# First two pairs' carry and values in smaller steps, third pair's loads moved ahead of the second weights, every order anew

## The chip, the cores and the metric

The kernel runs on one core of a Trainium2 chip. The core has five engines that run side by side: TensorE (PE, matmuls; PEld is its weight load), VectorE (DVE), ScalarE (ACT), GpSimd (POOL) and SyncE (SP). SP and GpSimd issue DMAs. Times are device microseconds (us); lower is better. The kernel before takes 174.0 us, the median of three runs (173.99 to 175.69).

## What is computed

Inputs are q, k, v and alpha, each of 4 batches, 8 heads, 768 positions and 48 dimensions, and two weights, w_in (384 x 2048) and w_out (2048 x 384). The first half is a recurrence with a decay:

```python
for t in range(S):
    state = alpha[:, :, t, :, None] * state + einsum('bhd,bhe->bhde', k[:, :, t], v[:, :, t])
    y[:, :, t] = einsum('bhd,bhde->bhe', q[:, :, t], state)
```

Its output, 3072 tokens of 384, goes through a two-layer network: `h = x @ w_in; g = relu(h) ** 2; out = g @ w_out`.

## The kernel before

**Tiles.** Positions are cut into chunks of 128, and two chunks make a pair (256 positions of one batch, all heads). There are 12 pairs, three to a batch. Within a chunk, two neighbouring positions share a partition (i = 0, 1), so a chunk has 64 rows of two.

**A pair's stages, with the lines of the profile.** `loads` (L609, or L605 on GpSimd's queue) fetches alpha, k, q and v into RAW. `decay` takes the logarithm of alpha (ACT), sums it along the positions by matmuls with triangular ones, and takes the exponential of plus and minus the sums (asb); DVE multiplies q and k with it into QKS. For pairs 0 and 1 this is `decay_half`, in two halves of four heads (X = 0, 1): L675, L681, L693, L696; the others use L632 to L663. `values` casts v to bf16 into VBF (L624). `turned` transposes QKS into QKT: pairs 0 and 1 by halves on TensorE (L747), with an eviction by ACT (L758) or DVE (L761); pairs 2 and 3 in one piece (L715, L720); pairs 4 to 11 by a DMA (L727). `scores` multiplies q and k of a chunk (L777) into four banks (i, X); DVE multiplies each with the causal mask into PMB (L797), or ACT first evicts it to SBUF (L790) and DVE masks from there (L792). `carry` builds the state after each chunk: a matmul of k and v (L816), then DVE or GpSimd adds the old state and applies the chunk's decay (L831, L834, L837) into SBF. `mixed` makes the pair's output: the values, that is the masked scores times v (L856, the function `mm`, 48 matmuls for all heads), then the products of the old state (`before`, in two steps), then the eviction into XT (L903 by ACT, L900 by DVE). Pairs 4 to 11 use `mixed_back` (L932, L942) and a transposing DMA.

**The network.** `up` has eight steps per pair (u = 0 to 7): six matmuls of 256 columns (L985), relu on ACT (L995), the square on DVE into GT (L997). `down` has eight steps per pair, two halves of 128 tokens by four parts of four matmuls of 384 columns (L1018); after the fourth part ACT evicts (L1025) and a DMA stores. The last half of the last pair is `last_down` (L1037). `up` alternates between two PSUM banks (psH); the first WIDE steps, counted over all pairs, also take one of the two banks of `down` (psO). GT has three buffers.

**What sets the order.** Each stage has a number in TABLE, to which twice the pair's index is added; this is its priority. A planner in the program (`Program.order`) goes through the work engine by engine with costs written into each `add`, and of the operations that are ready takes the one of the lowest number; its result is the fixed order of instructions of each engine. Every engine then waits by semaphores for what it needs. Operations with dependencies across engines name what they read and write. The planner also puts matmuls on nothing (L1004, tile WARM) into idle time of TensorE before the first down.

**DMA order.** SP loads the first two pairs: alpha, k, q, v of pair 0, then of pair 1. GpSimd's queue holds the weights, cut into pieces: five of w_in (two of 2, three of 4 blocks of 128 columns) and four of w_out. PARTS says how they are dealt out: the first run waits for pair 1's alpha, and QUEUED puts pair 2's four loads on the same queue behind the first run. In the kernel before, the first run is six pieces (all of w_in and the first of w_out), then pair 2, then three pieces of w_out. OPENS lets pair 3's first load wait for one named piece.

Of the kernel before, what the change touches and what calls it, by code (L numbers as in the profile page):

```python
# [16 lines left out]
    dict(decay0=-97.00571, decay1=-78.81219, turned0=-80.03886, turned1=-50.01967, scores0=-30.48193, scores1=-47.68772, carry=-27.42287, mixed=-10.34508, up=13.54943, down=5.38323, scale00=46.21211, scale01=15.6952, scale10=-43.7223, scale11=24.38742, ends=-0.19963, values=-0.27295, loads=-207.65325, pair=-201.56601, last=-192.65267),  # L17
    dict(decay0=-75.64812, decay1=-42.50964, turned0=-47.6396, turned1=-36.35059, scores0=-27.54796, scores1=-14.27818, carry=-27.02336, mixed=-9.92749, up=13.91788, down=5.77749, scale00=24.25062, scale01=-73.05864, scale10=28.44156, scale11=53.47468, ends=69.1898, values=-2.51561, loads=-194.30495, pair=-191.20832, last=-172.89529),
    dict(decay=-7.48475, turned=3.12884, scores0=9.47855, scores1=6.55405, carry=1.85699, mixed=10.59462, up=17.47201, down=3.43096, loads=-74.75818),
    dict(decay=9.05655, turned=9.43988, scores0=10.08163, scores1=11.32914, carry=10.39665, mixed=11.89133, up=17.92099, down=4.23853, loads=-73.80479),  # L20
    dict(decay=9.3345, turned=9.43988, scores0=11.74226, scores1=10.89073, carry=10.54465, mixed=12.03376, up=21.0863, down=1.87816, loads=-73.8231),
    dict(decay=8.7564, turned=9.67304, scores0=11.70712, scores1=12.0564, carry=10.89438, mixed=12.21007, up=21.29448, down=1.43236, loads=6.43356),
    dict(decay=8.69387, turned=9.58387, scores0=11.86871, scores1=11.0227, carry=10.77621, mixed=11.96308, up=21.05913, down=2.40841, loads=7.7569),
    dict(decay=9.23435, turned=10.31244, scores0=11.36545, scores1=11.31146, carry=10.85231, mixed=12.13782, up=22.61627, down=2.40841, loads=8.07049),
    dict(decay=9.1013, turned=10.6921, scores0=11.60211, scores1=13.72977, carry=10.17742, mixed=18.09191, up=22.49685, down=2.4227, loads=7.9898),
    dict(decay=9.1013, turned=10.66148, scores0=19.46122, scores1=19.67082, carry=16.52927, mixed=20.05528, up=26.04938, down=2.38036, loads=7.9898),
    dict(decay=17.68176, turned=18.97432, scores0=20.03114, scores1=21.47118, carry=18.7218, mixed=19.83455, up=26.32882, down=2.72559, loads=13.16964, masks=-27.17958),
    dict(decay=17.68176, turned=18.97432, scores0=20.03114, scores1=21.47118, carry=18.7218, mixed=19.83455, up=26.32882, down=2.72559, loads=13.16964),
]
POOLS = [dict(decay=1, turned=2, scores=2, carry=1, mixed=2), dict(decay=0, turned=1, scores=1, carry=1, mixed=0)]  # L30
# [12 lines left out]
XTS = ('DVE', 'DVE')  # L43
COPIED = ((1,), (2,))
TURNS = ('DVE', 'ACT')
# [385 lines left out]
def bass_gla_recurrent__then__act_relu_squared_kernel(  # L431
# [23 lines left out]
    KT = DM // 128  # L455
# [213 lines left out]
    def decay_half(g, X, at):  # L669

        r, l, a, x, c_ = g % NRAW, g % NLAB, g % NASB, g % NQK, g % NAC
        ps, key = bank(POOLS[g]["decay"])
# [59 lines left out]
    def turned_half(g, X, at):  # L732

        x, t = g % NQK, g % NQT
        if g == 0:
            spots = [bank(POOLS[g]["turned"]) for z in range(2)]
        else:
            spots = [bank(POOLS[g]["turned"])] * 2
# [27 lines left out]
    def scores(g, at, js=range(NP), late=0.0):  # L766
        t, m = g % NQT, g % NPM
        halves = sorted({j // 2 for j in js})
        banks = {(i, X): bank(POOLS[g]["scores"] if g < FIRST else 0) for X in halves for i in range(2)}
# [35 lines left out]
    def carry(g, at, spots=None):  # L805
        x, vb, c_ = g % NQK, g % NV, g % NAC
        first, final = g % NW == 0, g % NW == NW - 1
        chunks = [0] if final else [0, 1]
        banks = [pr.bank(spots or pools[POOLS[g]["carry"] if g < FIRST else 0]) for c in chunks]

        def mm(pe):
# [9 lines left out]
        add("PE", mm, 250, at, reads=[("qks", x, 0, X) for X in range(2)] + [("vbf", vb)],  # L821
            writes=[b[1] for b in banks], form=64, size=32 * len(chunks))
# [21 lines left out]
    def mixed(g, at, spots=None, between=None):  # L844
# [29 lines left out]
        def mm(pe):  # L874
            order = [[s for s in shares if s[1] % 2 == col] for col in range(2)]
            for y in range(2 * KT):
                for i in range(2):
                    for col in range(2):
                        h, n, off = order[col][y]
# [176 lines left out]
    for g in range(G):  # L1056
# [15 lines left out]
        if g - 1 not in RUNS:  # L1072
            stage(2 * g + o["carry"], lambda at, g=g: carry(g, at), "carry", g)
# [138 lines left out]
```

## Time and profile before

| | us |
|---|---|
| median of three runs | 174.0 |
| lowest and highest | 173.99, 175.69 |
| the profiled execution | 174.21 |
| its span, first to last instruction | 172.5 |
| TensorE busy | 167.6 |
| VectorE busy | 119.4 |
| ScalarE busy | 116.9 |
| GpSimd busy | 36.4 |

The granted TensorE clock is full in nearly the whole span. In the page's groups a line reads: source line, engine, operation, output and inputs by name, shapes, count; then the busy time of the group and the mean of one instruction; then the idle time of that engine ahead of these instructions and what ended it. In an answer in order of time, the first number is the start, the second the length. The chain of work that ended last is followed back from the last instruction to what released each step.

### The profile page before, as it was taken

The page shows a single profiled execution, that of the slowest core. Times are in us where ns is not written, and L with a number is a line of the kernel's source. Part 1 is how long each engine was busy: PE and PEld are TensorE (multiplying, and loading weights), DVE is VectorE, ACT ScalarE, POOL GpSimd, SP SyncE. Part 2 cuts the span into 40 slices and gives each one's busy share as a digit, 9 for nine tenths or more (in the row PEclk, how much of TensorE's full clock was granted, in tenths as well). Part 3 has the DMA queues.
Part 4 walks back from the last instruction along what each step waited for, and adds up shares of the span by engine and source line. Part 5 has one row for each costly group of instructions (what it writes and reads, how often), then busy time and mean ns, then how long its engine had stood idle before and what let it go on. Part 6 is the DMA issues. An engine that isn't in the chain of part 4 may idle for free.

```text
span 172.5 us, 6016 instructions
## 1 busy us (share of the span) xinstructions
PE 167.6 (97%) x2611; PEld 123.9 (72%) x2611; DVE 119.4 (69%) x257; ACT 116.9 (68%) x236; POOL 36.4 (21%) x63
## 2 busy tenths in 40 slices
PE   7889999999999999999999999999999999999994
PEld 7457687757777786777777777777776867877763
DVE  7887958964999999578897698289784804423300
ACT  2887679546989685568993794669973556657621
POOL 4079600100012001010142122320512310202220
PEclk9999999999999999999999999999999999999999
DMA  5999999999994999999999999999929343112122
GB/s 138 323 304 171 206 324 238 157 270 287 308 327 113 230 217 261 144 305 196 323 203 234 218 207 252 236 231 332 186 50 160 72 62 62 22 25 49 40 51 91
DMA packets 76314, 32.89 MB, mean 191 GB/s; under 512 B 69632, under 2 KB 75456, under 8 KB 76288
## 3 DMA queue, kind: packets, MB, share of 16 engines
q1 hardware_dynamic: 70384, 25.04, 65.0%
q0 software_dynamic: 5904, 7.47, 21.8%
q8 instruction: 20, 0.33, 0.8%
q14 instruction: 6, 0.05, 0.1%
HBM read 25.17 MB, written 4.72 MB: 173 GB/s over the span
## 4 chain that ended last, share of the span: by engine, by line
PE 95%; DVE 2%; issue 1%; ACT 0%
PE psH L985 36%; PE psO L1018 36%; PE psG L777 4%; PE psO L1004 3%; PE psG L856 2%; PE psG L942 2%; PE psG L816 2%; PE psO L1037 2%; PE psG L932 2%; PE psO L985 2%; DVE qks L696 2%; PE psG L642 1%; PE psG L715 1%; PE psG L681 1%; PE psH L856 1%
## 5 line engine op out<-in xcount | busy, mean ns | idle before, releaser
L995 ACT ACTIVATE rr<-psH 128x512 bf16<-128x512 f32 x92 | 55.3, 612 | 22.6 <-PE psH L985 20.6
L985 PE MATMUL psH<-xt,win 128*128 128x256 bf16 x552 | 70.5, 273 | 0.0
L1018 PE MATMUL psO<-wout,gt 128*128 128x384 bf16 x368 | 70.0, 326 | 0.0
L985 PEld LDWEIGHTS psH<-xt,win 128*128 128x128 bf16 x552 | 52.7, 98 | 11.6 <-DVE xt L900 0.2
L997 DVE TENSOR_TENSOR gt<-rr 128x512 bf16<-128x512 bf16 x96 | 40.3, 434 | 29.6 <-ACT rr L995 29.3
L1018 PEld LDWEIGHTS psO<-wout,gt 128*128 128x128 bf16 x368 | 34.3, 98 | 17.8 <-ACT osb L1025 0.3
L797 DVE TENSOR_TENSOR pm<-psG,mask 128x512 bf16<-128x512 f32 x44 | 27.9, 682 | 3.7 <-PE psG L777 2.9
L971 POOL DMA_DIRECT2D out_dram<-osb x28 | 15.0, 541 | 47.4 <-ACT osb L1025 47.4
L837 POOL TENSOR_TENSOR sbf<-ust,acp 128x192 bf16<-128x192 f32 x13 | 9.0, 689 | 75.3 <-DVE ust L834 75.2
L1025 ACT ACTIVATE osb<-psO 128x384 f32<-128x384 f32 x23 | 11.3, 492 | 14.6 <-PE psO L1018 14.3
L663 DVE TENSOR_TENSOR qks<-raw,asb 128x768 bf16<-128x768 f32 x20 | 18.7, 966 | 2.0 <-ACT asb L652 2.0
L632 DVE TENSOR_TENSOR raw<-raw 128x384 f32<-128x384 f32 x20 | 11.0, 564 | 0.0
L624 ACT ACTIVATE vbf<-raw 128x768 bf16<-128x768 f32 x12 | 10.1, 842 | 0.0
L652 ACT ACTIVATE asb<-psG 128x384 bf16<-128x384 f32 x20 | 9.9, 497 | 0.2
L958 ACT ACTIVATE yb<-psG 128x384 bf16<-128x384 f32 x14 | 6.2, 489 | 4.4 <-PE psG L932 4.4
L777 PEld LDWEIGHTS psG<-qkt 64*64 64x64 bf16 x360 | 5.7, 106 | 4.0 <-issue 2.8
L1004 PE MATMUL psO<-warm 128*128 128x128 bf16 (+1 forms) x41 | 7.4, 347 | 1.1 <-DVE warm L523 1.1
L777 PE MATMUL psG<-qkt 64*64 64x128 bf16 x360 | 8.3, 220 | 0.1
L632 DVE TENSOR_TENSOR raw<-raw,ro 128x384 f32<-128x384 f32 x10 | 5.5, 551 | 0.8 <-DMA raw<-in_q_dram 0.5
L648 ACT ACTIVATE ro<-raw 128x384 f32<-128x384 f32 x10 | 5.2, 524 | 0.6 <-DMA raw<-in_alpha_dram 0.6
L834 DVE TENSOR_TENSOR ust<-psG,sbf 128x192 f32<-128x192 f32 x14 | 4.9, 353 | 0.7 <-POOL sbf L837 0.4
L654 ACT ACTIVATE ro<-ro 128x384 f32<-128x384 f32 x10 | 5.2, 524 | 0.1
(104 smaller groups left out, 137.2 us busy)
## 6 DMA issues: line engine op xcount, KB each, us to landing
raw<-in_alpha_dram SPq DMA_DIRECT2D x11, 384.0 KB, 4.8
raw<-in_k_dram SPq DMA_DIRECT2D x11, 384.0 KB, 5.0
raw<-in_q_dram SPq DMA_DIRECT2D x11, 384.0 KB, 5.6
raw<-in_v_dram SPq DMA_DIRECT2D x11, 384.0 KB, 5.9
out_dram<-osb POOLq DMA_DIRECT2D x28, 96.0 KB, 2.6
out_dram<-osb SPq DMA_DIRECT2D x9, 192.0 KB, 3.9
wout<-in_moe_w_out_dram POOLq DMA_DIRECT2D x4, 384.0 KB, 13.6
win<-in_moe_w_in_dram POOLq DMA_DIRECT2D x3, 384.0 KB, 8.8
```

Of the source, the lines that this page charges most:

```text
L624: add("ACT", lambda act: act.activation(dst, src, AF.Copy), 740, at, reads=raw(r, 2), writes=[("vbf", vb)])
L632: add("DVE", lambda e: e.tensor_tensor(dst, a0, a1, ALU.mult), 470, at_, reads=reads, writes=writes, port=True)
L663: add("DVE", lambda dve, z=z, decays=decays: dve.tensor_tensor(QKS[x][:, z, :, :, 0:D], both(r, z), decays, ALU.mult), 870, at + 0.05 + 0. ...
L777: last = pe.matmul(banks[i, j // 2][0][64 * c:64 * c + 64, col:col + 128].rearrange("p (a b) -> p a b", a=2), QKT[t][64 * i:64 * i + 64, 0 ...
L797: add("DVE", lambda dve, i=i, X=X, ps=ps: dve.tensor_tensor(PMB[m][:, i, 2 * X:2 * X + 2].rearrange("p j n s -> p j (n s)"), ps[:].rearran ...
L971: add(by, lambda e, dst=dst, ps=ps: e.dma_start(dst, OSB[o][ps, :]), 600, at + 0.01 * i, reads=[("osb", o)], dma=("own" if by == "POOL" el ...
L985: last = pe.matmul(ps[:, f * TW:(f + 1) * TW].rearrange("p (c t) -> p c t", c=2), WIN[:, kt, fj * 128:(fj + 1) * 128], XT[:, 2 * (g % NX): ...
L995: add("ACT", lambda act: act.activation(ro, ri, AF.Relu), 480, at, reads=[key], writes=[key, ("rr", r)])
L997: add("DVE", lambda dve: dve.tensor_tensor(gt[:, 2 * u:2 * u + 2, :], rr, rr, ALU.mult), 340, at, reads=[("rr", r)], writes=[("gt", g % NG ...
L1004: last = pe.matmul(psO[1][:, 0:128 * wide].rearrange("p (a b) -> p a b", a=wide), WARM[:], bass.AP(tensor=WARM, offset=0, ap=[[128, 128], ...
L1018: last = pe.matmul(ps[:, 0:DM], GT[g % NGT][:, fj, tt * 128:(tt + 1) * 128], WOUT[:, fj, :], start=(fj == 0), stop=(fj == FT - 1))
L1025: add("ACT", lambda act: act.activation(OSB[o][:], ps[:, 0:DM], AF.Copy), 372, at, reads=[key], writes=[key, ("osb", o)])
```

## The change

- `carry` of pairs 0 and 1 becomes two stages, one for each chunk (PARTED), each with its own matmul group, bank and priority (carry and carry1).
- The values of pairs 0 and 1 become two groups of 24 matmuls, one for heads 0 to 3, which reads the masked scores of X = 0, and one for heads 4 to 7 (HALVED).
- COPIED: two of the four score banks of pairs 0 and 1 are evicted by ACT and masked from SBUF, where one was: X = 1 for pair 0, X = 0 for pair 1.
- CASTS: pair 0's v is cast by GpSimd in place of ACT; the code makes this wait for pair 0's QKS. TURNS: the second half of pair 1's transposes is evicted by DVE in place of ACT.
- PARTS: the first run of weights is the five pieces of w_in; then come pair 2's loads, then all four pieces of w_out. OPENS: pair 3's first load waits for the last piece of w_out, where it waited for the one before it.
- WIDE goes from 10 to 14, BEHIND[7] from 6 to 4 (pair 7's loads are queued behind pair 4's transposing DMA), the banks of the first two pairs get a choice for each half (POOLS), and every number of TABLE and WEIGHTS is new.

```diff
-WEIGHTS = (-75.27555, -73.28278)
+WEIGHTS = (-342.59653, -175.33888)
-BEHIND = {6: 4, 7: 6, 8: 6, 9: 7, 10: 7, 11: 9}
+BEHIND = {6: 4, 7: 4, 8: 6, 9: 7, 10: 7, 11: 9}
-WIDE = 10
-PARTS = ((1, 3, 6), (2, -1, 3))
-OPENS = {3: 7}
+WIDE = 14
+PARTS = ((1, 3, 5), (2, -1, 4))
+OPENS = {3: 8}
-CASTS = ('ACT', 'ACT')
+CASTS = ('POOL', 'ACT')
-COPIED = ((1,), (2,))
-TURNS = ('DVE', 'ACT')
+COPIED = ((2, 3), (0, 1))
+TURNS = ('DVE', 'DVE')
+PARTED = (1, 1)
+HALVED = (1, 1)
...
-    def carry(g, at, spots=None):
+    def carry(g, at, spots=None, part=None):
...
-        chunks = [0] if final else [0, 1]
-        banks = [pr.bank(spots or pools[POOLS[g]["carry"] if g < FIRST else 0]) for c in chunks]
+        chunks = [0] if final else [0, 1] if part is None else [part]
+        name = "carry1" if part else "carry"
+        banks = {c: pr.bank(spots or pools[POOLS[g][name] if g < FIRST else 0]) for c in chunks}
...
-        add("PE", mm, 672, at, reads=[("vbf", vb)] + [("pm", m, i, X) for i in range(2) for X in range(2)],
-            writes=[b[1] for b in banks], form=64, size=96)
+        if g < FIRST and HALVED[g]:
+            for Y in range(2):
+                add("PE", lambda pe, Y=Y: mm(pe, range(4 * Y, 4 * Y + 4)), 450, at + 0.001 * Y,
+                    reads=[("vbf", vb)] + [("pm", m, i, Y) for i in range(2)],
+                    writes=[b[1] for b in banks], form=64, size=48)
+        else:
+            add("PE", mm, 672, at, reads=[("vbf", vb)] + [("pm", m, i, X) for i in range(2) for X in range(2)],
+                writes=[b[1] for b in banks], form=64, size=96)
...
+            if g < FIRST and PARTED[g]:
+                for c in range(2):
+                    stage(2 * g + o["carry1" if c else "carry"], lambda at, g=g, c=c: carry(g, at, None, c), "carry", g, c)
+            else:
+                stage(2 * g + o["carry"], lambda at, g=g: carry(g, at), "carry", g)
```

In the table, the priorities of pairs 0 to 3 before and after, twice the index added: the carry of pair 0 was -27.4, behind its scores (-30.5, -47.7); it is now -349.3 and -243.7, ahead of them (-158.6, -228.2). Of pair 2, decay to scores were -3.5 to 13.5 with ups of pair 0 from 13.5; they are now -57.8 to -34.6, with ups of pair 0 from -44.1.

More of the change, by code (lines that the diff above doesn't have):

```diff
@@ L768, in scores @@
         halves = sorted({j // 2 for j in js})
-        banks = {(i, X): bank(POOLS[g]["scores"] if g < FIRST else 0) for X in halves for i in range(2)}
+        banks = {(i, X): bank(POOLS[g]["scores%d" % X] if g < FIRST else 0) for X in halves for i in range(2)}
         def mm(pe):
@@ L820, in mm @@
             return last
-        add("PE", mm, 250, at, reads=[("qks", x, 0, X) for X in range(2)] + [("vbf", vb)],
-            writes=[b[1] for b in banks], form=64, size=32 * len(chunks))
+        add("PE", mm, 250 if part is None else 260, at, reads=[("qks", x, 0, X) for X in range(2)] + [("vbf", vb)],
+            writes=[b[1] for b in banks.values()], form=64, size=32 * len(chunks))
         for c in chunks:
@@ L1116, in bass_gla_recurrent__then__act_relu_squared_kernel @@
             ahead(("decay", g, 0), [("decay", g, 1)])
+            if PARTED[g]:
+                ahead(("carry", g, 0), [("carry", g, 1)])
         ahead(("turned", g), [("decay", g + NQK)])
```

41 lines of the change are left out of this document (21 added, 20 removed).

## The prediction

> **What bounds the kernel now.** I read the page first: span, busy times and the chain that ended last.
>
> ```profile
> span 172.5 us, 6016 instructions
> PE 167.6 (97%) x2611; PEld 123.9 (72%) x2611; DVE 119.4 (69%) x257; ACT 116.9 (68%) x236; POOL 36.4 (21%) x63
> PE 95%; DVE 2%; issue 1%; ACT 0%
> ```
>
> TensorE holds 95% of the chain; VectorE and ScalarE have about 30% to spare. So the time is the TensorE work, which this change hardly touches, plus whatever time TensorE loses. The chain in order of time says where it loses any (start, duration, what).
>
> ```profile
> 13.08 0.80 PE psH L856 x48
> 14.43 0.37 PE psG L816 x32
> 16.06 0.32 PE psO L1004
> 16.74 0.83 PE psH L985 x6
> 20.66 0.32 issue
> 24.04 1.31 PE psH L985 x12
> 27.32 0.65 PE psO L1018 x4
> 32.52 1.00 PE psG L715 x16
> ```
>
> L985 is an up step (6 matmuls, 1.31 / 2 = 0.655 us each), L1018 a down step (4 matmuls, 0.65 us), L856 the end products and values of pairs 0 and 1, L816 the carry of the state, L1004 a filler that computes nothing. The first up starts at 16.74. From 24.04 on I see no idle piece of any weight in this chain: one TensorE step follows the next to the end. What can be won is therefore the head, and it must be won as up and down steps that run earlier. The windows on L985 (two rows) and on L1018 (one) count those.
>
> ```profile
> 0.00:24.00 24.00, 5.24 (x44) 3.99 (x45) 1.00 1.09 237
> 0.00:29.00 29.00, 9.76 (x83) 7.88 (x84) 1.00 1.09 245
> 0.00:29.00 29.00, 0.81 (x4) 0.39 (x4) 1.00 1.09 245
> ```
>
> At 24 us TensorE has started 44 / 6 = 7.3 ups; at 29 us 83 / 6 = 13.8 ups and one down. Pairs 0 and 1 together have only 16 ups. That ceiling matters below.
>
> **Part 1, pair 0: carry by chunk, values by halves.** In order of time, the engines behind the first up:
>
> ```profile
> 14.87 0.36 DVE L831 TENSOR_TENSOR sbf<-psG,acp 128x192 bf16<-128x192 f32 x1 [0.97 <-PE psG L816]
> 16.09 0.59 DVE L900 CAST xt<-psH 128x384 bf16<-128x384 f32 x1
> 22.86 0.59 ACT L903 ACTIVATE xt<-psG 128x384 bf16<-128x384 f32 x1
> ```
>
> Pair 0's values end at 13.08 + 0.80 = 13.88, but its x is complete only at 16.09 + 0.59 = 16.68: the carry runs at 14.43, its state is ready at 14.87 + 0.36 = 15.23, and the products of the old state still follow. With the carry by chunk in its new place (ahead of the scores and the mixing in the table) the state exists before the masks end, so 15.23 - 13.88 = 1.35 us of this falls away. Values by halves let four heads run while the last masks are made: at most half of 0.80, 0.40 us more. So x of pair 0 is complete at about 15.0 to 15.3. What a carry of one chunk takes, no row shows; between half of 0.37 and the full 0.37. I take the full one, as its 32 matmuls lose their neighbours in the array: 4 x 0.37 - 2 x 0.37 = 0.74 us more TensorE over the two pairs. It lies in the filler's place (16.06 and before) and costs nothing there; without that cover 0.74 us.
>
> **Part 2, masks, copies and the cast.** The prices, from the groups by line and the order of time:
>
> ```profile
> L797 DVE TENSOR_TENSOR pm<-psG,mask 128x512 bf16<-128x512 f32 x4 | 2.6, 681 | 0.5 <-PE psH L777 0.5
> L792 DVE TENSOR_TENSOR pm<-rr,mask 128x512 bf16<-128x512 bf16 x2 | 0.8, 416 | 0.0
> L790 ACT ACTIVATE rr<-psH 128x512 bf16<-128x512 f32 x1 | 0.6, 615 | 0.0
> L624 ACT ACTIVATE vbf<-raw 128x768 bf16<-128x768 f32 x2 | 1.7, 845 | 0.0
> L758 ACT ACTIVATE qkt<-psG 128x1024 bf16<-128x1024 bf16 x2 | 2.1, 1026 | 0.6 <-PE psG L747 0.6
> 33.16 1.28 DVE L720 COPY qkt<-psG 128x1024 bf16<-128x1024 bf16 x2
> L837 POOL TENSOR_TENSOR sbf<-ust,acp 128x192 bf16<-128x192 f32 x13 | 9.0, 689 | 75.3 <-DVE ust L834 75.2
> L542 POOL TENSOR_SCALAR_AFFINE_SELECT mask<-mask 64x256 bf16<-64x256 bf16 x2 | 0.8, 413 | 0.1
> ```
>
> One more mask per pair through an eviction: VectorE saves 0.681 - 0.416 = 0.27, ScalarE pays 0.62. Pair 1's second transposed half moves from ScalarE (1.03) to VectorE (1.28 / 2 = 0.64). Pair 0's cast leaves ScalarE (0.85). Over the head ScalarE wins 1.03 + 0.85 - 2 x 0.62 = 0.64, VectorE pays 0.64 - 2 x 0.27 = 0.10. Both lie beside waits.
>
> The cast on GpSimd has no row. By the selection it is 3 x 0.41 = 1.24 us for 768 columns, by the product 4 x 0.69 = 2.76; it has one input as the selection has, so I take 1.3. The code lets it start once pair 0's four scaled quarters of q and k are done; behind it on GpSimd's queue stand all weight loads. Its user is the carry.
>
> The Trainium skill (SBUF — State Buffer, section "SBUF: two separate sides") has GpSimd and VectorE share a pair of ports as an exclusive lock held for a whole instruction, also against VectorE operations with two SBUF inputs. No run shown here has the two side by side; by that rule the cast also holds up VectorE's products for up to its own length, and the sum below would be 1.2 us at best and 0.1 us below nothing at worst.
>
> **Part 3, third pair's loads ahead of wout.** GpSimd's issues with their starts, each followed by its time to landing; then the answer on the tile wout.
>
> ```profile
> 9.50 0.91 POOL L579 DMA_DIRECT2D win<-in_moe_w_in_dram  x1 [5.95 <-DMA raw<-in_alpha_dram]
> win<-in_moe_w_in_dram POOLq DMA_DIRECT2D x1, 192.0 KB, 5.3
> 12.73 0.77 POOL L579 DMA_DIRECT2D win<-in_moe_w_in_dram  x1
> win<-in_moe_w_in_dram POOLq DMA_DIRECT2D x2, 384.0 KB, 9.2
> 13.50 0.78 POOL L581 DMA_DIRECT2D wout<-in_moe_w_out_dram  x1
> wout<-in_moe_w_out_dram POOLq DMA_DIRECT2D x1, 384.0 KB, 10.8
> 16.91 0.91 POOL L605 DMA_DIRECT2D raw<-in_v_dram  x1
> raw<-in_v_dram POOLq DMA_DIRECT2D x1, 384.0 KB, 12.1
> L581 POOL DMA_DIRECT2D wout<-in_moe_w_out_dram x4: 780/802/806, 13.5 to 19.3; - x4
> DMA to landing us min/median/max: 10.8/13.6/15.4
> ```
>
> Landings now: first win 14.8, last win about 12.73 + 9.4 = 22.1, first wout 24.3, the third pair's v 29.0, last wout 19.3 + 15.4 = 34.7. The stream is the same bytes in another order. So the first wout lands where v does now, 29.0, and the third pair about 24.3 - 22.1 = 2.2 us earlier each, v near 26.8; the last wout stays at 34.7. The fourth pair's alpha, which waits for the third wout piece now and for the last then, goes about 2 us later; its ups come after those of the third pair, which were not due until long after, so I price it at nothing (2 us at most, if TensorE runs dry).
> The first down, now at 27.32, cannot start before 29.0: from about 22 to 29 TensorE has only ups and the third pair to live on. If the cast delays the first win issue (9.50), all these landings slip by it: nothing to 2.8 us by the two prices above. The first row says that GpSimd idles 5.95 us ahead of that issue, and most of the cast fits in there, so I take 0.5.
>
> **Can ScalarE feed that?** Two windows of all engines (PE, PEld, DVE, ACT, POOL busy):
>
> ```profile
> 15.00:20.00 5.00, 4.98 (x103) 3.41 (x101) 4.81 (x13) 2.91 (x6) 5.00 (x7) 1.00 1.22 198
> 20.00:25.00 5.00, 4.66 (x101) 3.80 (x102) 3.09 (x8) 3.60 (x7) 0.07 (x1) 1.00 1.19 283
> L995 ACT ACTIVATE rr<-psH 128x512 bf16<-128x512 f32 x10 | 5.8, 597 | 1.5 <-PE psH L985 1.3
> ```
>
> ScalarE idles 2.09 + 1.40 = 3.49 us there, and gets 0.64 more; 2.2 further ups take 1.3, so 2.8 us are left for the third pair's logarithms and exponentials. Enough, but an up costs ScalarE 0.597 of TensorE's 0.655: while only ups run, it is 91% taken and every other ScalarE operation pushes them back.
>
> **The sum, as TensorE's ledger at 29 us.** Pair 1's x, ready now at 22.86 + 0.59 = 23.45, comes some 2 to 3 us earlier (1.35 + 0.40 from pair 0 and masks that no longer wait behind it). That is enough for all 16 ups by 29: gain 2.2 x 0.655 = 1.45. The down that cannot start: -0.65. The third pair, 2.2 us earlier, can have its transposes (1.00) and carry (0.37) done by then, work that now comes at 32: between 0 and 1.37, I take 0.9. The later win (0.5) goes off: 1.45 - 0.65 + 0.9 - 0.5 = 1.2 us. After 29 each wout piece frees two downs of 0.65, and the rest of the third pair fills between; I see no loss. So 174.21 - 1.2 = 173.0 for an execution like the profiled one (174.21, of which 172.5 is span), and 0.2 less on the median of the runs shown, 174.0: **172.8 us**.
>
> **Rivals.**
> - *The head gains in full.* The third pair's work fits, the cast delays nothing, pair 1 is 3 us earlier: 1.45 - 0.65 + 1.37, and the 0.74 stays hidden, plus up to 0.6 of filler and issue gaps (rows 16.06 and 20.66): 2.8 us, 171.2. For it: TensorE computed nothing useful in much of the first 24 us. Against: 16 ups are all there is until 29.0.
> - *Nothing arrives earlier where it counts.* Ups of pair 0 go on waiting for win (22.1 for the last quarter), and what is won in pair 1 is lost to the missing down: 174.0, between -0.7 and +0.7.
> - *Starved before wout: slower.* The mechanism is the stretch 22 to 29 without a down. If ScalarE takes the third pair's logarithms first (as the new table ranks them), ups come at its pace; 3 us of such work ahead of them is 3 us in which TensorE has banks but no evictions. It decides once more than 1.5 us of it falls into the stretch; at 3 us, with the win 0.5 late: 176.0. For it: 91%. Against: 2.8 us of slack.
> - *The new order makes a later pair wait.* Every priority from pair 2 to 11 changes and the seventh pair's loads follow another transpose. Now the chain has no idle after 24 us; a late transfer for one pair would open a gap of one to several us: 176.5. For it, only that nothing of the new order is in the trace.
> - *Code loading.* Rows for it:
>
> ```profile
> PEld psG L856 <- issue: 0.7, 2, 0.5
> q8 instruction: 20, 0.33, 0.8%
> ```
>
> TensorE waited 0.7 us in L856 for nothing the profile shows, amid full DMA queues. The new order packs more small matmuls before 24 us; if these are code loads, each one more costs about 0.35, and 3 of them leave 173.9, the second rival's time. The Trainium skill (Runtime: NRT & Kernel Launch, "Instruction fetch mechanics") says 16 KiB blocks are fetched ahead and mostly hidden; by that rule this falls away, though the trace's 20 packets of 0.33 MB fit such blocks and its 0.7 us of issue is not explained by it.
>
> **Chances and range.** Forecast (172.3 to 173.7) 0.38; full gain 0.24; nothing, code loading with it, 0.14; starved 0.13; later wait 0.11. One per cent, 1.74 us, is about what a measurement of this kernel can tell from no change. Faster by over that: the full gain and a part of the forecast's lower end, 0.30. Slower by over it: nearly all of the two slow cases, 0.24 less a part that stays small: 0.22. Within: 0.48. The range reaches from 170.9 (the full gain and its last tenths) to 176.3 (the starved case and half of the later wait), with some 0.12 out above and 0.04 below. The likeliest case alone is 172.3 to 173.7.
>
> **What would show it.** Right: first L985 at about 15, pair 1's x near 21, 15 to 16 ups and no down at 29, first L1018 just after 29, no idle in TensorE's chain from 21 on, win landings within 0.5 us of now. Wrong: the cast ending after 10.5, first win issue with it; fillers or idle between 22 and 33; ScalarE's window 20 to 30 full while TensorE waits for L995; any wait of TensorE for a load or transpose after 35.

## The result and the profile after

On one chip, twelve runs of each kernel, the changed kernel takes 175.82 us in the median (175.16 to 177.88) and the kernel before 174.65 (173.96 to 176.06). The ratio is 1.0062, with a 95% interval from 1.0033 to 1.0091: about 1.1 us slower (0.62% of 174.65), where 1.2 us faster was forecast. It leaves out the two slowest runs of the changed kernel (177.84 and 177.88). The profiled executions stand at 175.71 and 174.21, their spans at 174.0 and 172.5.

The page of the changed kernel: span, busy times, and the share of the engines in the chain that ended last.

```profile
span 174.0 us, 5998 instructions
PE 168.3 (97%) x2605; PEld 124.7 (72%) x2605; DVE 120.1 (69%) x258; ACT 115.0 (66%) x236; POOL 37.5 (22%) x64
PE 85%; DMA 8%; ACT 3%; POOL 1%; DVE 1%; issue 1%
```

TensorE holds 85% of the chain, where it held 95%, and transfers have 8%. TensorE is busy 0.7 us longer with 6 matmuls fewer, and the other engines got little more to do. So time went into waits and into slower steps of TensorE. Lines moved by the edit: L985 (up) is now L996, L1018 (down) L1029, L856 (values and old state of pairs 0 to 3) L859, L816 (carry) L819, L777 (scores) L779.

The head first: windows of the changed kernel on L996 (two rows) and on L1029 (one), length and TensorE busy with the count of matmuls.

```profile
0.00:24.00 24.00, 5.31 (x43) 3.83 (x44) 1.00 1.07 250
0.00:29.00 29.00, 10.04 (x84) 7.83 (x85) 1.00 1.10 246
0.00:29.00 29.00, 0.00 (x0) 0.00 (x0) 1.00 1.10 246
```

By 29 us 84 up matmuls have started, where it was 83, and no down, where it was 4. The first ups do start earlier. From the order of time of the changed kernel (start, length, engine, line, operation):

```profile
8.38 0.82 POOL L623 CAST vbf<-raw 128x768 bf16<-128x768 f32 x1 [4.81 <-DVE qks L698]
13.80 0.59 DVE L911 CAST xt<-psO 128x384 bf16<-128x384 f32 x1
...
22.95 0.60 ACT L914 ACTIVATE xt<-psG 128x384 bf16<-128x384 f32 x1
...
30.36 0.61 PE L717 MATMUL psG<-ident,qks 128*128 128x128 bf16 x8
30.80 0.81 PE L1029 MATMUL psO<-wout,gt 128*128 128x384 bf16 x4
```

Pair 0's x is complete at 13.80 + 0.59 = 14.39 (16.68 before). Pair 1's is complete at 23.55 (23.45 before). So 2.3 us won at pair 0 are gone at pair 1. Pair 1's masks and the start of its values show where most of it went, first in the kernel before, then in the changed one:

```profile
16.84 1.27 DVE L797 TENSOR_TENSOR pm<-psG,mask 128x512 bf16<-128x512 f32 x2
19.55 0.41 DVE L792 TENSOR_TENSOR pm<-rr,mask 128x512 bf16<-128x512 bf16 x1
20.02 0.64 PE L856 MATMUL psG<-pm,vbf 64*64 64x128 bf16 x32
```

```profile
16.86 1.28 DVE L799 TENSOR_TENSOR pm<-psG,mask 128x512 bf16<-128x512 f32 x2
18.06 0.75 DVE L794 TENSOR_TENSOR pm<-rr,mask 128x512 bf16<-128x512 bf16 x2
18.05 1.47 PE L996 MATMUL psH<-xt,win 128*128 128x256 bf16 x12 [0.44 <-DMA win<-in_moe_w_in_dram]
19.45 0.86 PE L859 MATMUL psG<-pm,vbf 64*64 64x128 bf16 x38
```

Pair 1's masks begin at 16.86, where they began at 16.84. Their scores (L779) run at 16.21, behind pair 0's first up, where they ran at 16.31, and VectorE does the four steps of pair 1's carry ahead of them, until 16.9; so pair 0's earlier x did not bring them forward. Two of the masks now come by way of ScalarE, and the last ends 1.15 us earlier (18.81 for 19.96). The values start only 0.57 us earlier, because two ups stand ahead of them on TensorE and wait for win until 18.05.

Now the waits. Of the waits of TensorE and of the chain of the changed kernel:

```profile
PE psG L859 <- issue: 0.7, 1, 0.7
PE psG L779 <- DMA qkt<-qks: 0.5, 1, 0.5
PE psH L996 <- DMA win<-in_moe_w_in_dram: 0.4, 1, 0.4
```

```profile
11.09 6.83 DMA win<-in_moe_w_in_dram
...
20.31 0.71 issue
21.02 0.64 PE psG L859 x20
...
89.63 6.64 DMA qkt<-qks
...
96.32 0.64 PE psG L779 x32
```

Three places are to be seen: a wait for the third piece of win (landed at 11.09 + 6.83 = 17.92), an idle piece with no releaser at 20.31, and pair 7's transposing DMA, issued at 89.63 and waited for until 96.32 (in the kernel before it was issued at 83.62, and its scores started at 91.82 with no wait).

**The ledger.** I took the start-to-start distances of all TensorE matmuls in both traces. At 22.56 us before and 22.65 us after, both have the same things behind them: five ups, and pair 1's values and old-state products. From there to the end of TensorE's last matmul it is 147.50 us before and 148.91 us after. So the head lost 0.09 us, and 1.41 us were lost behind it, in the same number of ups and downs. Of these, 0.58 is pair 7's transfer: the step from a down to the scores at 95.48 takes 0.84 us, where such a step without a wait takes 0.26. Nearly all of the rest has no wait. What differs is how often TensorE goes between 128-row matmuls (ups, downs, sums) and 64-row ones (scores, carry, values): behind 22.6 us it runs 24 separate stretches of 64-row matmuls before and 27 after. One example, pair 3's output and pair 4's carry, in the chain of the kernel before and then of the changed one:

```profile
52.68 0.79 PE psG L856 x48
...
53.64 0.25 PE psG L816 x22
53.89 0.18 PE psG L856 x6
54.07 0.76 PE psO L1018 x4
```

```profile
53.77 0.96 PE psG L859 x54
54.73 0.76 PE psO L1029 x4
55.49 0.29 PE psG L859 x6
55.78 0.76 PE psO L1029 x4
56.53 0.37 PE psG L819 x32
56.90 1.42 PE psH L996 x12
```

Before, pair 3's values and old state and pair 4's carry are one stretch of 52.68 to 54.07. After, they are three, and each down behind one takes 0.76 where a down behind a down or an up takes 0.65; the pair of ups takes 1.42, where 1.31 is usual. What such a break costs was measured (the last two runs below): 0.22 us, so three more make 0.66. The ledger has it too: in both traces the step into a 64-row stretch takes 0.09 us more than the usual distance behind that matmul, and the step out of it 0.13. So 0.58 + 0.66 = 1.24 of the 1.41 are accounted for; a single step at 28.14, from the third pair's sums to an up, has another 0.17, with no releaser shown.

### The profile page after: what moved, and what is told of

It reads as the page before. It is cut to its first block, busy times and chain, and to the rows that moved or that the text cites. A ratio compares the mean times of both kernels' runs of the same rounds, so it can differ in the third digit from the quotient of the medians.

```text
span 174.0 us, 5998 instructions
## 1 busy us (share of the span) xinstructions
PE 168.3 (97%) x2605; PEld 124.7 (72%) x2605; DVE 120.1 (69%) x258; ACT 115.0 (66%) x236; POOL 37.5 (22%) x64
## 4 chain that ended last, share of the span: by engine, by line
PE 85%; DMA 8%; ACT 3%; POOL 1%; DVE 1%; issue 1%
PE psO L1029 33%; PE psH L996 33%; DMA win<-in_moe_w_in_dram 4%; DMA qkt<-qks 4%; PE psG L779 3%; PE psG L859 2%; PE psO L1015 2%; PE psG L953 2%; PE psO L996 2%; PE psO L1048 2%; PE psG L819 2%; PE psG L943 1%; PE psG L717 1%; POOL win L581 1%; DVE qks L698 1%; ACT rr L1006 1%
## 5 line engine op out<-in xcount | busy, mean ns | idle before, releaser
L996 PE MATMUL psH<-xt,win 128*128 128x256 bf16 x546 | 69.1, 273 | 0.4 <-DMA win<-in_moe_w_in_dram 0.4
L1029 PE MATMUL psO<-wout,gt 128*128 128x384 bf16 x368 | 69.1, 326 | 0.0
L996 PEld LDWEIGHTS psH<-xt,win 128*128 128x128 bf16 x546 | 51.7, 98 | 10.9 <-issue 0.7
L1029 PEld LDWEIGHTS psO<-wout,gt 128*128 128x128 bf16 x368 | 34.4, 98 | 18.4
L1036 ACT ACTIVATE osb<-psO 128x384 f32<-128x384 f32 x23 | 11.3, 493 | 22.1 <-PE psO L1029 21.9
L634 DVE TENSOR_TENSOR raw<-raw 128x384 f32<-128x384 f32 x20 | 11.5, 585 | 1.5 <-DMA raw<-in_alpha_dram 0.8
L626 ACT ACTIVATE vbf<-raw 128x768 bf16<-128x768 f32 x11 | 9.3, 844 | 0.0
L779 PE MATMUL psG<-qkt 64*64 64x128 bf16 x376 | 8.3, 219 | 0.5 <-DMA qkt<-qks 0.5
L779 PEld LDWEIGHTS psG<-qkt 64*64 64x64 bf16 x376 | 5.9, 106 | 4.0 <-issue 2.3
L1015 PE MATMUL psO<-warm 128*128 128x128 bf16 (+1 forms) x35 | 5.9, 341 | 1.1 <-DVE warm L525 1.1
L634 DVE TENSOR_TENSOR raw<-raw,ro 128x384 f32<-128x384 f32 x10 | 6.2, 616 | 0.3 <-ACT ro L656 0.3
L819 PEld LDWEIGHTS psG<-vbf,qks 64*64 64x64 bf16 x288 | 4.3, 108 | 1.8 <-ACT vbf L626 0.7
L819 PE MATMUL psG<-vbf,qks 64*64 64x48 bf16 x288 | 5.5, 188 | 0.0
```

Of the source, the lines that this page charges most:

```text
L634: add("DVE", lambda e: e.tensor_tensor(dst, a0, a1, ALU.mult), 470, at_, reads=reads, writes=writes, port=True)
L779: last = pe.matmul(banks[i, j // 2][0][64 * c:64 * c + 64, col:col + 128].rearrange("p (a b) -> p a b", a=2), QKT[t][64 * i:64 * i + 64, 0 ...
L819: last = pe.matmul(banks[c][0][64 * i:64 * i + 64, j * D:(j + 1) * D], QKS[x][64 * c:64 * c + 64, 0, n, 2 * j + i, :], VBF[vb][64 * c:64 * ...
L996: last = pe.matmul(ps[:, f * TW:(f + 1) * TW].rearrange("p (c t) -> p c t", c=2), WIN[:, kt, fj * 128:(fj + 1) * 128], XT[:, 2 * (g % NX): ...
L1029: last = pe.matmul(ps[:, 0:DM], GT[g % NGT][:, fj, tt * 128:(tt + 1) * 128], WOUT[:, fj, :], start=(fj == 0), stop=(fj == FT - 1))
L1036: add("ACT", lambda act: act.activation(OSB[o][:], ps[:, 0:DM], AF.Copy), 372, at, reads=[key], writes=[key, ("osb", o)])
```

## The experiments

All edits are to the changed kernel, if nothing else is said; ratios are to the kernel before on the same chip, with their 95% intervals.

**1. Two downs ahead of pair 7's scores.** The fixed order of TensorE is changed behind the planner: the two down steps that follow pair 7's scores go ahead of them, to cover the transfer.

```diff
     pr.order(downs)
+    for seq in (pr.programs["PE"], pr.sequence):
+        late = [o for o in seq if o.eng == "PE" and (o.stage or ())[:2] == ("scores", 7)]
...
+        seq[at:at] = two
```

> The changed kernel with one edit: the two down steps that stand behind the scores of the eighth pair (pair 7) are put ahead of them on TensorE; all else is in the same order. In the changed kernel TensorE waits there 0.68 us (95.41 + 0.16 to 96.25) for that pair's transposing DMA. Theory A (the time lost behind 22.6 us is in part this wait): the wait goes, the down steps fill it, and the time falls by 0.5 to 0.7 us, to a ratio to the kernel before of about 1.003. Rival (the transfer would only be late elsewhere, or the wait is hidden by slack): time unchanged, ratio 1.006, a new wait behind 97 us.

Ratio 1.0063 [1.0039, 1.0086]. Waits of TensorE in this run:

```profile
PE psG L859 <- issue: 0.7, 1, 0.7
PE psG L644 <- DVE pm L799: 0.6, 1, 0.6
```

The wait for the DMA is gone, and pair 8's sums now wait 0.6 us for pair 7's masks instead (at 98.24), as the rival had it: the scores were late, and what was put ahead of them was missing behind them. Covering the wait with work that was needed anyway was worth nothing here.

**2. Shorter warm-up.** 7 warm-up matmuls of 512 columns in place of 28 of 128: the same columns in 42 recorded instructions fewer, the order unchanged.

```diff
-    add("PE", lambda pe: busy(pe, WARMUP[0], WARMUP[1]), 2950, -6, reads=["warm"], writes=[("psO", 1)], size=2 * WARMUP[0],
+    add("PE", lambda pe: busy(pe, 7, 4), 2950, -6, reads=["warm"], writes=[("psO", 1)], size=2 * WARMUP[0],
```

> The changed kernel with its 28 warm-up matmuls of 128 columns as 7 of 512 columns: 42 TensorE instructions fewer, the same order of everything else. Theory B (TensorE's head is paced by blocks of 256 instructions of its code; the third such block comes in at about 20.97 us in the kernel before and in the changed one, both at their 705th instruction): the wait of 0.9 us at the 38th matmul of pair 1's values (20.03 to 20.96) leaves that place, and a wait appears 42 instructions later, in pair 1's products of the old state or the up after them, ending at 21 to 22 us. Since the block is only asked for later too, the time changes little: between -0.4 and +0.3 us. Rival (the wait is one for masks, banks or the split of the values): it stays at the same matmul and ends at 20.97.

Ratio 1.0069 [1.0047, 1.0092]. In order of time:

```profile
20.11 0.36 PE L859 MATMUL psG<-qkt,sbf 64*64 64x128 bf16 x9
21.18 0.21 PE L859 MATMUL psG<-qkt,sbf 64*64 64x128 bf16 x1 [0.71 <-issue]
```

The idle piece came behind the 38th matmul of pair 1's values; now it comes behind 48 of them and 11 old-state products, 21 matmuls and 21 weight loads later. It belongs to a place in the instruction stream, the 705th recorded TensorE instruction (matmuls, weight loads and waits for semaphores) in this trace, in the changed kernel and in the kernel before, and not to an operand or a bank. It ends at nearly the same time (21.18, where it was 21.02; the expectation counts the changed kernel's times from 0.07 us later), and the total doesn't change.

**3. More small warm-ups.** 98 instructions more at the start, 57 of the warm-ups as 64x64.

```diff
-    add("PE", lambda pe: busy(pe, WARMUP[0], WARMUP[1]), 2950, -6, reads=["warm"], writes=[("psO", 1)], size=2 * WARMUP[0],
+    add("PE", lambda pe: [busy(pe, 20, 1), *(pe.matmul(psO[n % 2][64 * (n // 2 % 2):64 * (n // 2 % 2) + 64, 0:64], WARM[64 * (n % 2):64 * (n % 2) + 64, 0:64], WARM[64 * (n % 2):64 * (n % 2) + 64, 0:64]) for n in range(57))][-1], 2950, -6, reads=["warm"], writes=[("psO", 0), ("psO", 1)], size=2 * WARMUP[0],
```

> The changed kernel with 98 more TensorE instructions before the first load lands (20 warm-up matmuls of 128 columns and 57 small ones of 64 by 64 in place of 28), the same order of everything else. Theory B: the limits between blocks of code move 98 instructions forward in the work, so the wait of 0.9 us inside pair 1's values goes, and the next limit falls at about the up step that waits for the third piece of w_in anyway (17.27 to 17.98 us); pair 1's x comes 0.5 to 0.9 us earlier, the ups behind it too, and the time falls by 0.3 to 0.8 us although TensorE gets more to do. Rival (no code loading; the wait belongs to the values): the wait stays at the 38th matmul of the values and the time stays or grows by up to 0.5 us.

Ratio 1.0223 [1.0181, 1.0266], and inconclusive: the page's row of granted clock in 40 slices shows another cause at work.

```profile
PEclk9975999999999999999999999999999999999999
```

A slice is 177.1 / 40 = 4.4 us long. The clock falls to 0.7 in the third (8.9 to 13.3 us) and 0.5 in the fourth (to 17.7), and the first up starts at 18.75, 3.3 us late. What the place of the code blocks would have done to the time cannot be told from it.

**4. Values undivided.** Only the split of the values by halves of the heads is undone; the planned order stays the same.

```diff
-HALVED = (1, 1)
+HALVED = (0, 0)
```

> The changed kernel with the values of pairs 0 and 1 in one group again, waiting for all four masks; the planned order is the same. Theory B: at 22.6 us the head stands where it stood, since the block of code comes at 20.97 either way; time within 0.2 us. Rival C (the two groups cost TensorE time, 0.2 us and more for each pair, or cause the wait inside the values): faster by 0.4 us or more. Rival D (the split is worth what it was meant to be): slower by 0.4 us or more.

Ratio 1.0058 [1.0036, 1.008], the changed kernel's own. In order of time:

```profile
19.16 0.75 PE L859 MATMUL psG<-pm,vbf 64*64 64x128 bf16 x38
21.09 0.35 PE L859 MATMUL psG<-pm,vbf 64*64 64x128 bf16 x10 [1.19 <-issue]
```

TensorE starts these 38 matmuls 0.3 us earlier than in the changed kernel (19.45) and goes on no earlier (21.09, where it was 21.02): the idle piece grows from 0.71 to 1.19. What is won ahead of it is taken there. The split is worth nothing here: the expectation held, and both rivals fall.

**5. Pair 7 earlier by its priorities.**

```diff
-    dict(decay=16.22963, turned=16.89477, scores0=18.25529, scores1=17.78853, carry=17.20085, mixed=18.86262, up=27.87705, down=1.73749, loads=15.0968),
+    dict(decay=10.6, turned=11.0, scores0=18.25529, scores1=17.78853, carry=17.20085, mixed=18.86262, up=27.87705, down=1.73749, loads=9.0),
```

> The changed kernel with the eighth pair's (pair 7) loads, decay and transposing DMA given earlier priorities (loads 9.0, decay 10.6, turned 11.0 in place of 15.1, 16.2, 16.9); up to about 75 us the order stays, behind it TensorE's order changes by the planner. Theory A2 (the new order of the later pairs brings pair 7's scaled q and k too late, and putting other steps first only moved the wait by 1 us): with the transfer issued some us earlier no TensorE wait is left at 95 to 98 us, and the time falls by 0.4 to 0.8 us, ratio 1.002 to 1.004. Rival (the wait is not what costs; the switches between matmul groups do): ratio stays at 1.006.

Ratio 1.0304 [1.0266, 1.0342]. In order of time:

```profile
88.99 0.83 PE L779 MATMUL psG<-qkt 64*64 64x128 bf16 x32 [1.27 <-DMA qkt<-qks]
```

A new number makes the planner place everything behind it anew. The wait for a transposing DMA became longer (1.27 us at 88.99), others came at 90.2 and 122.4 us (0.4 and 0.2), and TensorE has 31 stretches of 64-row matmuls behind the head (27 in the changed kernel). The expectation failed, and the run says little of the transfer itself; run 9 does by hand what this one meant.

**6. The later pairs' old priorities.** All parts of the change, but the ten rows of TABLE for pairs 2 to 11 as before, pair 7's loads behind pair 6 again, and the second run of weights just behind the third pair's loads.

```diff
-BEHIND = {6: 4, 7: 4, 8: 6, 9: 7, 10: 7, 11: 9}
+BEHIND = {6: 4, 7: 6, 8: 6, 9: 7, 10: 7, 11: 9}
-WEIGHTS = (-342.59653, -175.33888)
+WEIGHTS = (-342.59653, -74.55)
...
```

> The changed kernel with all its parts and the first two pairs' new priorities, but with the rows of the third pair and all later ones (and the seventh pair's loads) as in the kernel before; the second run of weights moves just behind the third pair's loads, as its order wants. Theory A2 (all 1.4 us are lost behind 22.6 us, by the later pairs' order): ratio 0.998 to 1.002, and no TensorE wait behind 30 us. Rival E (the parts themselves cost it, through the later first down and the third pair's loads ahead of wout): ratio 1.004 to 1.010, TensorE losing between 22 and 45 us.

Ratio 1.025 [1.0204, 1.0297]. Waits of TensorE:

```profile
PE psH L996 <- ACT xt L914: 0.8, 1, 0.8
PE psG L644 <- DVE pm L799: 0.8, 1, 0.8
```

Both lie between 42 and 47 us, behind the third pair; later than that TensorE waits for nothing. The expectation failed, and the loss is larger than its rival had it, too. So the old order has no wait for pair 7, but it has these two, and 29 stretches of 64-row matmuls behind the head. That it doesn't fit a head in which the first down and pair 3's loads come later is my reading; no run tests it.

**7. All parts, all priorities of before.** The whole TABLE is that of before, and so is the queueing of pair 7's loads; carry1 of pairs 0 and 1 comes right behind carry.

```diff
...
-WEIGHTS = (-342.59653, -175.33888)
+WEIGHTS = (-75.27555, -73.28278)
```

> All parts of the change with every priority as in the kernel before, the carry's two stages next to each other where the one was. Theory B (code loading paces the head) and A2: the head at 22.6 us stands within 0.5 us of the kernel before, later pairs as before: ratio 0.998 to 1.004. Rival E: ratio 1.005 or more. If the parts are worth 1 us and only their order spoilt it: 0.994 or less.

Ratio 1.0238 [1.0193, 1.0283]. Waits of TensorE:

```profile
PE psG L859 <- issue: 1.9, 1, 1.9
```

The expectation failed: the parts without an order made for them lose 4 us. The idle piece at the 705th instruction, which TensorE reaches at 19.7 and leaves at 21.8, has 1.9 us, where the kernel before has 0.3.

**8. Order alone.** The new priorities, all parts off, WIDE and the weights' order of before.

```diff
-PARTS = ((1, 3, 5), (2, -1, 4))
+PARTS = ((1, 3, 6), (2, -1, 3))
-CASTS = ('POOL', 'ACT')
+CASTS = ('ACT', 'ACT')
-PARTED = (1, 1)
-HALVED = (1, 1)
+PARTED = (0, 0)
+HALVED = (0, 0)
...
```

> The changed kernel's priorities and banks alone: carry and values in one piece, masks, casts, evictions and the order of the weights as in the kernel before. Theory A2: still slower than the kernel before, ratio 1.003 or more, with TensorE waits behind 60 us. Rival E: ratio 1.000 within 0.002.

Ratio 1.0166 [1.0125, 1.0208]. Waits of TensorE:

```profile
PE psG L779 <- DMA qkt<-qks: 0.6, 1, 0.6
PE psO L996 <- DMA win<-in_moe_w_in_dram: 0.6, 1, 0.6
```

The expectation held: slower, with the wait for a transposing DMA at 120.8 us. This head reaches the common point at 22.44 us, no later than the other two, and TensorE needs 3.1 us more than the kernel before from there to its end, with 29 stretches of 64-row matmuls for 24. Taken together, 6 to 8 say that neither half of the change can be priced alone: order and parts belong together, and each without the other costs 1.7 to 2.5%. They don't divide the 0.6%; run 8 shows that the new order loses behind the head without any of the parts.

**9. Pair 7's transfer earlier, by hand.** The planned order stays, and only the steps ahead of this DMA are moved up: on TensorE the sums ahead of two ups, on ScalarE two exponentials ahead of two relus, on VectorE two products ahead of two squares and a product of pair 8. (`ahead(engine, stage, at, n)` moves the next n operations of a stage directly in front of the first one of another.)

```diff
     pr.order(downs)
+    ahead("PE", ("decay", 7, 0), ("up", 5, 0), 1)
+    ahead("ACT", ("decay", 7, 0), ("up", 5, 0), 2)
+    ahead("DVE", ("decay", 7, 0), ("up", 5, 0), 2)
```

> The changed kernel with pair 7's chain to its transposing DMA put some steps earlier in the fixed order and nothing else: on TensorE its sums ahead of the two ups in front of them, on ScalarE its two exponentials ahead of the two relus, on VectorE its two products ahead of a square, a product of pair 8 and another square. Theory: TensorE's wait for this DMA before pair 7's scores (0.5 us by the waits, 0.68 by the starts) is half of the loss. Then the DMA is issued about 1.2 us earlier (88.4), lands near 95.1, the wait is gone and the time falls by 0.6 to 0.7 us, to a ratio of 1.002 to 1.003 against the kernel before. Rival: the downs, whose squares now come 1.8 us later, or pair 7's masks wait instead, as in the run with the two downs put first; then the wait shows up at another line between 86 and 100 us and the ratio stays at 1.006.

Ratio 1.0032 [1.0004, 1.0061]. In order of time, SyncE's queue and TensorE:

```profile
88.28 2.01 SPq L729 DMA_TRANSPOSE qkt<-qks  x1
...
95.52 0.64 PE L779 MATMUL psG<-qkt 64*64 64x128 bf16 x32
...
115.08 0.49 PE L996 MATMUL psH<-xt,win 128*128 128x256 bf16 x3 [0.41 <-issue]
```

The DMA is issued 1.35 us earlier (89.63 before), the scores start with no wait at 95.52 in place of 96.32, and nothing else waits between 86 and 100 us. Half of the loss is gone by the ratios (0.0062 to 0.0032; the intervals overlap, so the trace is the better evidence). In the ledger the step to pair 7's scores is 0.59 us shorter, the whole of what the transfer had cost. The trace also shows where it was lost again: at 109 us TensorE is 0.79 us ahead of the changed kernel, at 119 us 0.22. Between lies an idle piece with no releaser in an up step, 0.58 us above the usual distance, at the 3777th recorded instruction of TensorE; 3777 is 705 + 12 x 256. The twelve times of this run fall into two groups, 174.4 to 174.7 (five) and 175.3 to 176.0 (seven, the profiled one among them). Whether that block is late in the second group alone, one profile can't say.

**10. The kernel before with the short warm-up.**

```diff
-    add("PE", lambda pe: busy(pe, WARMUP[0], WARMUP[1]), 2950, -6, reads=["warm"], writes=[("psO", 1)], size=2 * WARMUP[0],
+    add("PE", lambda pe: busy(pe, 7, 4), 2950, -6, reads=["warm"], writes=[("psO", 1)], size=2 * WARMUP[0],
```

> The kernel before with its warm-up in 7 matmuls of 512 columns in place of 28 of 128, so 42 recorded instructions fewer ahead of everything, same order. Theory: the code block sets the stall, so it moves 42 instructions later and stays about as long as the 0.48 us that it costs now; the time is the same within 0.3 us. Rival: before escapes the stall altogether, because its 705th instruction then comes when the block is there; then TensorE's idle piece at 20.66 is gone and the time is 0.4 to 0.5 us lower, a ratio of 0.997.

Ratio 1.0016 [0.9984, 1.0048]: no difference. In order of time:

```profile
20.51 0.27 PE L856 MATMUL psG<-qkt,sbf 64*64 64x128 bf16 x5
21.57 0.30 PE L856 MATMUL psG<-qkt,sbf 64*64 64x128 bf16 x7 [0.79 <-issue]
```

In the kernel before the idle piece came behind 32 of pair 1's 48 values; now it comes behind all 48 and 5 old-state products: again 21 matmuls, 42 instructions, later. Its place was expected; that it grew from 0.32 to 0.79 wasn't, and the rival of escaping it is refuted.

**11 and 12. The price of a break.** 96 small matmuls on zeros, which the reference doesn't need, are added among the last twelve downs, where TensorE works without a wait: in one block, and as twelve blocks of 8 (there the list is [8] * 12).

```diff
+    late = [o for o in pr.programs["PE"] if o in downs][-12:]
+    for o, n in zip(late, [96] + [0] * 11):
+        o.fn = lambda pe, f=o.fn, n=n: (small(pe, n), f(pe))[1]
```

> The changed kernel with 96 matmuls of 64x48 on zeros added in one block ahead of the twelfth down step from the end (they write a bank that is not used there; the output is untouched). By the carry's groups (32 in 0.25 us between their neighbours) this adds 0.75 us and one change to 64-row matmuls and back. Both theories expect this; it is the base of the next run.

> The same 96 matmuls dealt out as 8 ahead of each of the last twelve down steps: twelve changes to 64-row matmuls and back in place of one. Theory: each change costs about 0.1 us each way, or 0.2 for both, so this takes 11 x 0.1 to 11 x 0.2 = 1.1 to 2.2 us longer than the run before it, seen in the starts of the last down steps. Rival: a change costs nothing, and the longer sums of the split groups in the changed kernel come from elsewhere; then the last stretch of both runs is equal within 0.2 us.

Ratios 1.0137 [1.0064, 1.021] and 1.026 [1.0189, 1.0332], from two executions each; the traces say more. The chains, one block and then twelve (the first two of them):

```profile
161.83 0.89 PE psG L1178 x96
162.72 7.91 PE psO L1029 x48
```

```profile
160.91 0.18 PE psG L1178 x8
161.09 0.76 PE psO L1029 x4
161.84 0.18 PE psG L1178 x8
162.02 0.76 PE psO L1029 x4
```

From the start of the down ahead of the first block to the start of the last half (L1048) it is 8.45 us in the changed kernel (160.31 to 168.76), 9.45 with one block (161.02 to 170.47) and 11.86 with twelve (160.10 to 171.96). The same matmuls in eleven more blocks take 2.41 us more: 0.22 us for each change to 64-row matmuls and back, a little over the 0.1 to 0.2 expected. The down behind each block takes 0.76, not 0.65, as in the example above. The rival, that a change is free, is refuted. The Trainium skill (TensorEngine Tiling (Array Packing), section "Tiling Modes") says that a change of tiling mode drains TensorE; it gives no time. These two runs agree with it, at 0.22 us.

## Why the prediction was wrong, point by point

- **What bounds the kernel: right.** The time is TensorE's work and what it loses; all losses are read on TensorE.
- **Pair 0's x at 15.0 to 15.3: right in kind, even earlier.** 14.39; the first up starts at 15.45 (16.74 before, about 15 forecast).
- **The carry at 0.74 us more, hidden in the filler's place: right.** By the common point carries take 0.53 us more of TensorE and fillers 2.15 less. The rest of that room went to values and old state with the idle piece in them (0.80 more), to ups with their wait for win (0.50) and to pairs 0 and 1's sums (0.43).
- **The cast at 1.3, the later win at -0.5: too dear.** The cast took 0.82 and ended at 9.20; the first win issue came at 9.40 (9.50 before). That term is nothing. By the rule of the Trainium skill on the shared port (SBUF — State Buffer, "SBUF: two separate sides") VectorE's products might have been held up by as much. No run here shows it: pair 0's products ended at 8.31, ahead of the cast, which waits for them, pair 1's began at 11.06, and beside the cast stand two copies from PSUM of 0.42 us each, as long as before.
- **The landings: right.** First wout 28.8 (29.0 said), the third pair's v 27.1 (26.8), last wout 34.7 (34.7), last win 21.8 (22.1). But the first down started at 30.80, not just after 29.
- **Pair 1's x some 2 to 3 us earlier, enough for all 16 ups by 29 (+1.45): this failed first.** It came 0.1 us later; 84 / 6 = 14.0 ups had started. The term is worth 0.11 (one matmul). The step that failed is "1.35 + 0.40 from pair 0 and masks that no longer wait behind it": pair 1's masks began at 16.86, where they had begun at 16.84, and the ups ahead of its values waited for win. What was left of the gain, 0.35 us when TensorE came to its 705th instruction (20.10, 20.44 before), ended there: it went on at 21.02 in the one kernel and at 20.98 in the other.
- **-0.65 for the down: right to the matmul** (4 fewer by 29).
- **+0.9 for the third pair: 0.44.** Its sums (5 matmuls, 0.44 us) were done by 29; its transposes came at 30.36 and 31.45, its carry at 32.64. Half of the term was the guess that these fit as well.
- **The sum of 1.2: about 0.** 0.11 - 0.65 + 0.44 = -0.1, which agrees with the common point (22.65 after, 22.56 before). No fillers and no wait stand between 22 and 29, but for the 0.17 at 28.14: the starved case didn't happen.
- **"After 29 ... I see no loss": this failed second, and cost more.** 0.58 for pair 7's transfer, 0.66 for three more breaks. The sign "any wait of TensorE for a load or transpose after 35" came, at 95.8. The rival "the new order makes a later pair wait" had the place and the kind of the first, with a price of one to several us; the second was in no rival. I priced every operation by its own row and took the ups and downs as the same 0.65 wherever they stand; rows of 0.76 for a down and 1.42 for a pair of ups stood in the trace of before.
- **"Nothing arrives earlier where it counts": right for the head.** Pair 0's ups did wait for win (the row of 0.4), and the **code loading** counted with this rival took the last 0.35 us. But the mechanism wasn't "each one more": the stall comes where TensorE reaches a limit in its instructions too early, and it ends at a time that earlier work doesn't move. (The 0.7 us that the prediction quotes for it is the weight loads' row; TensorE's own idle time there was 0.32.)

**What the code blocks do.** The instruction queue moves 20 packets of 16,384 bytes in either trace. The records of that queue, beside the first TensorE instruction behind the limit (the 705th, or for the last row the 3777th):

| | last start ahead of it | packet starts | next instruction | from packet |
|---|---|---|---|---|
| before | 20.44 | 18.76 | 20.98 | 2.2 |
| after | 20.10 | 18.71 | 21.02 | 2.3 |
| short warm-up (2) | 20.25 | 18.82 | 21.18 | 2.4 |
| values undivided (4) | 19.69 | 18.79 | 21.09 | 2.3 |
| old priorities (7) | 19.68 | 19.32 | 21.77 | 2.5 |
| order alone (8), no idle time | 20.90 | 18.30 | 20.90 | 2.6 |
| before, short warm-up (10) | 20.57 | 19.03 | 21.57 | 2.5 |
| pair 7 by hand (9), at 3777 | 114.39 | 112.63 | 115.08 | 2.4 |

TensorE goes on 2.2 to 2.5 us after the packet's start, however early it came to the limit; in run 8, which came 2.6 us behind it, it didn't stop. Counted through all limits of the 14 traces, with every 256th instruction set beside the packet of its number, none starts less than 2.2 us behind its packet. The Trainium skill (Runtime: NRT & Kernel Launch, "Instruction fetch mechanics") has blocks of 16 KiB, 256 instructions, fetched ahead, and the cost of a boundary mostly hidden. The size agrees with the packets and with the distance of the two limits. Hidden it is at most limits, where TensorE's starts lie within 0.2 us of each other in both kernels; in the head, with the DMA queues full and TensorE in small matmuls, it is not: 0.71 us here, 1.9 in run 7. The changed kernel comes early to the limit before it too, the 449th: it lost 0.2 us there, in a filler at 14.4, ahead of the wait for win.

Not settled: what sets the start of a packet (in the table it comes 3 to 4.2 us after the limit before was passed, and no run tests it), and the 0.17 us at 28.14.

## What to carry to other kernels

An early end of one pair helps the next only where the next waits for it: look in the trace for what its own masks and values wait for. And a gain in the head counts only up to the next thing that has its own clock: look for an idle piece that nothing releases, count the instructions up to it, and ask whether earlier work can move its end. Price a new order by its neighbours too: count how often TensorE changes between 64-row and full matmuls (0.22 us each time there and back), and follow each transfer that is issued later to the work that needs it. To test one wait, move a few operations in the finished order; a changed priority plans everything anew and answers another question.

## What the runs showed of the hardware that I had not expected

- TensorE's instruction stream has limits every 256 instructions. At the one near 21 us it idled in 12 of the 14 traces, for 0.2 to 1.9 us; in run 8, which came there 2.6 us behind the packet, it didn't. In run 9 it idled at a later one too, 0.41 us by the trace's idle column.
- 96 matmuls of 64x48 in one block take about 0.78 us beside the change (1.00 us added by one block, less 0.22), or 8 ns each with four of them side by side; in blocks of 8 the change costs more than the 8 x 8 ns of work.
- When 57 of the warm-up matmuls were 64x64, the granted clock fell to 0.7 and then 0.5 between 9 and 18 us; with a warm-up of 28 matmuls of 128 columns (both kernels) or 7 of 512 (runs 2 and 10) it stayed full there.
